# Sliding-window attention and a gated convolution FFN: keys as pairs of tokens, attention in 64x64 tiles of the array

## The chip, the core and the metric

The program runs on one NeuronCore of one Trainium2 chip. The time is the device time of one execution, in microseconds (us). Five engines work beside each other, each through its own instructions in program order: PE (TensorE: matrix products, with weight loads as PEld), DVE (VectorE), ACT (ScalarE), POOL (GpSimd) and SP (SyncE, which here issues the DMAs). Sixteen DMA engines move the data. Products land in PSUM, which this kernel uses as eight banks of 128 x 512 floats.

## The reference

```python
# q, k, v: (8 batches, 8 heads, 576 tokens, 64), f32
scores = q @ k.T / 8                       # per batch and head
scores = where(|i - j| <= 32, scores, -1e9)
attn   = exp(scores - max) / (sum + 1e-9)
x      = (attn @ v), heads side by side    # (8, 576, 512)
h      = relu(x @ w_in)                    # w_in: 512 x 1024
conv_t = sum over kk of conv_w[kk] * h[t + kk - 1]   # 3 taps, per channel, zero at the ends
out    = (h * sigmoid(conv)) @ w_out       # w_out: 1024 x 512; out: (8, 576, 512), f32
```

## The kernel before

All products are in bf16. Queries stand in tiles of 64 tokens, nine per batch. A tile's queries see only the 128 keys from 32 before it to 32 behind it. Two tiles that follow each other make a unit; there are 36 units, of which units 4 and 6 are worked as two halves (4a, 4b, 6a, 6b). The FFN goes in 12 chunks of 384 tokens, three per two batches of 576.

The order of the work is written out by hand: `PLAN` is a list of step names, and each step emits its instructions on its engines in that order. A name may carry the PSUM banks after @ and the engine after / (A for ACT, D for DVE, P for POOL, S for SP). The steps are:

- `LQK`, `CQK`, `TR`, `EV`: load q or k, cast it to bf16 (`qkb`), transpose it on PE, copy it out of PSUM (`qkT`). Head dimensions stand on 64 partitions, two head groups e = 0, 1 above each other.
- `LV`, `CV`, `VO`: load v in five pieces of 128 tokens per batch (`vst`), cast it (`ve`; a 65th column of ones gives the sums), and copy it with a shift of 64 tokens (`vo`), since an odd tile's 128 keys begin in the middle of a piece.
- `SC`, `EX`, `MA`, `AV`, `NO`: a unit's scores (keys on 128 partitions, queries along the row), exponential on ACT, mask on DVE, values product, and norm on DVE (a reciprocal and a multiplication, for each of two head groups).
- `XT`, `XE`: transpose x on PE and copy it to `xT`. From unit 20 on (`UD = 20`; units count from 0) the 16 units to the end have `XD` instead, a DMA transpose on SP's queue.
- `PH`, `RE`: hidden products of a chunk, eight of 128 channels, and relu on ACT to `hh`.
- `RO`: rows of `hh` rotated by 32, 64 or 96 partitions, by DMA or by DVE copies (`RO.2`).
- `CO`, `TA`, `GA`: the convolution as 32x32 diagonal products on PE, tanh on ACT, gate on DVE (`gT`). CO c.0 and c.1 are the two halves of chunk c.
- `YY`, `YC`, `YS`: output products, copy out of PSUM, store.
- `F`: products with zeros on PE that keep it busy while the first loads come.

Every engine copy goes through `copy`, every product through `mm` or `turn_mm`, so the profile puts them on those helpers' lines (L368, L370, L372; L378; L381). One instruction per engine waits for whatever its data need, and everything behind it on that engine waits too. An `LV` waits until the cast of the same piece of the batch before has freed its place in `vst`.

Tile size in this text means the part of PE's array that a product uses: 128*128 (hidden, output, x), 64*128 (scores; transposes of q and k), 128*64 (values), 32*32 (convolution). The rows of the profile print it.

Of the kernel before, what the change touches and what calls it, by code (L numbers as in the profile page):

```python
# [12 lines left out]
ALU = mybir.AluOpType  # L13
# [8 lines left out]
UD = 20  # L22
# [48 lines left out]

def build(k):
# [22 lines left out]
    def load_qk(b, parts):  # L95
        early = b < HB
        for z in parts:
            for y in range(2):
# [6 lines left out]
                add(f"TR{b}.{y}{z}", {"PE": 0.32}, lambda e, a=(q, ps): k.turn(*a), r=[("qkb", q)], w=ps, alloc=ps, mode="r64")  # L105
# [4 lines left out]
    def load_v(b):  # L110
        for c in range(5):
            add(f"LV{b}.{c}", {"SP": 0.58}, lambda e, a=(b, c): k.load_v(*a), w=[("vst", c)],
                size=1.32 if 0 < c < 4 else 1.05, desc=1024 if 0 < c < 4 else 768)
            add(f"CV{b}.{c}", {"POOL": 0.6} if b > 1 else {"POOL": 0.6, "DVE": 0.35, "ACT": 0.5},
                lambda e, a=(b, c): k.cast_v(e, *a), r=[("vst", c)], w=[("ve", b % 2, c)], port=1)
        for cs in [(c,) for c in range(4)] if b == 0 else [(0, 1, 2, 3)]:
            for h in range(2):
                add(f"VO{b}.{h}{cs[0]}", {"DVE": 0.06 + 0.14 * len(cs)}, lambda e, a=(b, h, cs): k.shift_v(e, *a),
                    r=[("ve", b % 2, c + h) for c in cs], w=[("vo", b % 2, c, h) for c in cs], port=1)

    def attend(u, tls):
# [3 lines left out]
        for t in tls:  # L125
            b, lt = (2 * u + t) // 9, (2 * u + t) % 9
            for hf in range(2):
                if b >= HB or (lt < 5, lt > 3)[hf]:
                    qk += [("qkT", b % 2, y, hf, x) for y in range(2) for x in range(2)]
            vs += [("vo", b % 2, lt // 2, h) for h in range(2)] if lt % 2 else [("ve", b % 2, lt // 2)]  # L130
        nm = f"{u}" + ("" if len(tls) == 2 else "ab"[tls[0]])
        ps = [Slot(), Slot()]
        add(f"SC{nm}", {"PE": 0.3 * f}, lambda e, a=(u, tls, ps): k.scores(*a), r=qk, w=ps, alloc=ps, mode="r64")
        for g in range(2):
            add(f"EX{nm}.{g}", {"ACT": 0.05 + 0.427 * f}, lambda e, z=(u, tls, ps[g], a, g): k.exp(*z),
                r=[ps[g]], w=[("attn", a, g)], uses=[ps[g]])
        add(f"MA{nm}", {"DVE": 0.06 + 0.54 * f}, lambda e, z=(u, tls, a): k.mask_(*z),
            r=[("attn", a, 0), ("attn", a, 1), "mk"], w=[("attn", a, 0), ("attn", a, 1)], port=1)
        ps = [Slot(), Slot()]
        add(f"AV{nm}", {"PE": 0.3 * f}, lambda e, z=(u, tls, ps, a): k.values(*z),  # L140
            r=[("attn", a, 0), ("attn", a, 1)] + vs, w=ps, alloc=ps, mode="c64")
        for g in range(2):
            add(f"NO{nm}.{g}", {"DVE": 0.54}, lambda e, z=(u, tls, ps[g], x, g): k.norm(*z),
                r=[ps[g]], w=[("xn", x, g)], uses=[ps[g]])
        if u >= UD:
            add(f"XD{nm}", {"SP": 1.22}, lambda e, z=(u, x): k.turn_x_dma(*z), r=[("xn", x, 0), ("xn", x, 1)],
                w=[("xT", u // 9 % 2, 2 * (u % 9) + t) for t in tls], size=1.3, desc=512)
            return
        ps = Slot()
        add(f"XT{nm}", {"PE": 0.24}, lambda e, z=(u, tls, ps, x): k.turn_x(*z),  # L150
            r=[("xn", x, 0), ("xn", x, 1)], w=[ps], alloc=[ps], mode="f")
        add(f"XE{nm}", {"DVE": 0.34, "ACT": 0.48}, lambda e, z=(u, tls, ps): k.evac_x(e, *z),
            r=[ps], w=[("xT", u // 9 % 2, 2 * (u % 9) + t) for t in tls], uses=[ps])
# [7 lines left out]
    def ffn(c):  # L161
        kind = c % 3
        for j in JORD:
            for g in range(2):
                m = 2 * j + g
                for half in (0, 1) if c == 1 else (None,):
                    lo, hi = span(c, half)
                    xs = [("xT", c // 3 % 2, t) for t in range(lo // 64, (hi - 1) // 64 + 1)]
# [39 lines left out]
    add("MK", {"DVE": 2.4}, lambda e: k.consts(), w=["mk"])  # L208
# [28 lines left out]
LQK0.10 LQK0.00 LQK0.11 MK LQK0.01 CQK0.10/A LV0.2 F512@0 F512@0 F512@0 F512@0 F512@0 F512@0 F512@0 F512@0 F512@0  # L237
F512@0 TR0.10@01 LV0.3 EV0.100/A EV0.101/D LV0.1 CQK0.00/D F512@2 F512@2 F512@2 TR0.00@10 CQK0.11/P EV0.000/D
EV0.001/A F512@2 SC0@10 TR0.11@23 LQK1.10 EX0.0 SC1@45 EV0.110/D EV0.111/A CQK0.01/P EX1.1 EX1.0 F512@6 F512@6
TR0.01@52 LQK1.00 EV0.010/D EV0.011/A EX0.1 LV0.0 F512@6 SC3@52 CW@4 MA0 LWI2 EX3.0 SC2@03 DG LV0.4 SC4a@16 EX2.1  # L240
LWI3 EX3.1 CV0.2/D EX2.0 VO0.11 CV0.3/A MA3 LWI0 CQK1.10/A MA1 LWI1 MA2 CV0.1/A F512@7 F512@7 F512@7 F512@7 F512@7
F512@7 F512@7 F512@7 F512@7 F512@7 F512@7 F512@7 F512@7 F384@7 TR1.10@02 VO0.03 VO0.12 EV1.100/A VO0.02 CQK1.00/D
F512@7 F512@7 F256@7 AV2@43 EV1.101/A VO0.10 EX4a.0 VO0.01 TR1.00@05 CV0.0/A NO2.0 AV1@12 EX4a.1 VO0.00 EV1.000/A
NO2.1 F384@7 AV0@64 EV1.001/A NO1.1 XT2@3 NO1.0 SC6a@50 EX6a.1 CV0.4/P NO0.0 F512@7 F128@7 XT1@1 SC5@02 CWI2/P XE1/A
SC4b@67 EX5.0 VO0.13 XE2/A CWI3/D LQK1.11 F512@1 F512@1 F128@1 AV3@01 EX5.1 MA4a EX4b.0 NO0.1 EX4b.1 LV1.0 NO3.1
F512@3 F512@3 F512@3 F512@3 XT0@4 LV1.3 NO3.0 AV4a@17 NO4a.1 XT3@0 XE0/D XE3/A CWI1/D EX6a.0 F512@3 F512@3 F512@3
F384@3 PH0.4@0 CWI0/P NO4a.0 LQK1.01 PH0.2@5 CQK1.11/P PH0.6@1 RE0.2 LV1.1 RE0.4 PH0.3@4 LV1.4 MA4b PH0.0@0 CV1.0/P
LV1.2 RE0.3 CV1.3/A PH0.1@5 MA5 RE0.6 MA6a AV4b@47 LV2.3 PH0.7@6 NO4b.1 LWO2 NO4b.0 TR1.11@12 CQK1.01/P XT4a@7
EV1.110/A EV1.111/D LWO1 XT4b@4 XE4a/A XE4b/D F512@3 F512@3 F128@3 TR1.01@21 RE0.1 LQK2.10 PH1.3a@7 RE0.0 EV1.011/D
EV1.010/A PH1.4a@5 RO0.1 CV1.4/P PH1.0a@0 CV1.1/A SC8@21 RE1.0a SC6b@43 EX8.0 CV1.2/D EX8.1 F512@0 F256@0 SC7@02  # L250
VO1.10 RE1.3a PH0.5@1 EX7.1 VO1.00 EX6b.0 PH1.6a@2 EX6b.1 MA8 EX7.0 AV5@47 MA6b PH1.5a@3 RE0.7 NO5.1 RE1.6a PH1.1a@0
RO0.3 RE1.5a NO5.0 AV6b@62 RE1.4a RE0.5 AV6a@37 PH1.2a@5 NO6b.0 XT5@1 LWO0 NO6a.1 PH1.7a@4 XE5/A NO6a.0 RE1.7a
F512@6 F128@6 AV8@67 RE1.1a MA7 RE1.2a XT6a@3 LWO3 CO0.0@5041 CWO1/P NO8.0 XE6a/A NO6b.1 AV7@63 TA0.03 NO8.1
PH1.5b@2 TA0.00 LQK2.00 NO7.1 CQK2.10 TA0.01 PH1.6b@7 RE1.5b NO7.0 RE1.6b XT6b@3 XT8@2 LQK2.11 GA0.01 CV2.3 XE6b/A
PH1.4b@7 XT7@6 XE8/D TA0.02 PH1.3b@0 RO0.2/D XE7/A PH1.1b@3 PH1.0b@2 RE1.4b RE1.1b GA0.00 PH2.4@6 RE1.0b RE1.3b
GA0.02 CO0.1@2537 GA0.03 PH1.2b@4 CWO0/P TA0.10 PH2.7@1 TA0.11 GA0.10 RE1.2b PH1.7b@0 TA0.12 CWO2/P GA0.11 RO1.1
PH2.3@4 RE2.4 GA0.12 RE2.7 PH2.6@5 RE1.7b CWO3/P TA0.13 RO1.3 PH2.5@0 GA0.13 CO1.0@1362 RE2.5 LQK2.01 RE2.6
TR2.10@07 CQK2.00 LV2.1 TA1.00 YY0.2@5 RE2.3 LV2.0 GA1.00 EV2.101/A EV2.100/D TA1.02 TA1.03 LV2.2 RO1.2/D CO1.1@0714
# [60 lines left out]
class Kernel:  # L319
# [54 lines left out]
    def fill(self, n, at):  # L374
        self.mm(self.banks[at][:, 0:n], self.zz[:, 0:128], self.zz[:, 0:n], start=True, stop=True)
# [343 lines left out]
```

## Time and profile before

| | us |
|---|---|
| three runs: median (lowest to highest) | 232.76 (232.06 to 235.51) |
| profiled execution: its time | 233.4 |
| profiled execution: span from first to last instruction | 231.7 |
| PE, DVE, ACT, POOL busy | 210.8, 173.3, 166.4, 64.4 |
| mean granted TensorE clock | 0.978 of full |
| DMA: data moved, share of 16 engines on the main queue | 48.80 MB, 78.2% |

Busy is the union of an engine's instructions. PE's instructions carry their way through the array, so that a busy PE may still have room, and two that follow each other overlap; steps on PE are better read from start to start. A row of the grouped views has line, engine, operation, output<-input, shapes and count, then busy us and mean ns of one, then the idle time ahead of it and what ended it. Some matmul records are missing from the trace, a few per cent.

### The profile page before, as it was taken

To read this page: it belongs to the slowest core of one execution; us is meant where nothing else is said; L and a number is where in the kernel's file an instruction comes from. 1 tells how busy PE (TensorE), PEld (TensorE's weight loads), DVE (VectorE), ACT (ScalarE), POOL (GpSimd) and SP (SyncE) were. 2 spreads that over 40 slices of the span, in tenths; PEclk is the share of its full clock that TensorE was granted. 3 is DMA by queue.
4 is the path that set the end of the run, shared out by engine and by line. 5 is a ranking of instruction groups with operands and counts; after the bars stand their busy time and mean duration, and the time that the engine had idled before them with its cause. 6 is when DMAs were issued, how large, how long until landed. Compare 5 with 4: busy or idle time off the path is not lost.

```text
span 231.7 us, 8843 instructions
## 1 busy us (share of the span) xinstructions
PE 210.8 (91%) x3705; PEld 122.0 (53%) x3737; DVE 173.3 (75%) x407; ACT 166.4 (72%) x365; POOL 64.4 (28%) x75
## 2 busy tenths in 40 slices
PE   7479898979999899899999999799899999899994
PEld 2354655756454665555455656455454655445543
DVE  7358874986779899958969888957799888643631
ACT  3366857867886899677796989798826877656861
POOL 2110443046345530555345114114043020000000
PEclk9957999999999999999999999999999999999999
DMA  5999949998899899994994696697996933621435
GB/s 161 321 267 266 296 108 229 236 274 257 218 280 316 244 226 340 257 273 122 344 329 67 208 236 202 171 229 120 362 221 109 260 132 79 190 57 37 160 118 201
DMA packets 67180, 49.38 MB, mean 213 GB/s; under 512 B 48044, under 2 KB 53444, under 8 KB 67140
## 3 DMA queue, kind: packets, MB, share of 16 engines
q1 hardware_dynamic: 67104, 48.80, 78.2%
q8 instruction: 29, 0.48, 0.9%
q14 instruction: 11, 0.09, 0.1%
q10 hardware_dynamic: 36, 0.01, 0.0%
HBM read 32.52 MB, written 9.44 MB: 181 GB/s over the span
## 4 chain that ended last, share of the span: by engine, by line
PE 49%; DVE 15%; DMA 12%; ACT 11%; issue 6%; SPq 4%; POOL 2%; DVEq 0%; ACTq 0%; POOLq 0%
PE ps L378 46%; ACT attn L520 6%; DMA hh<-hh 6%; DVE attn L528 4%; DMA vst<-in_v_dram 4%; DVE xn L549 4%; PE ps L381 3%; DMA st<-in_k_dram 3%; SPq L436 2%; ACT hh L596 2%; ACT qkT L368 2%; DVE gT L636 1%; DVE hh L370 1%; POOL ve L372 1%; DVE qkT L370 1%
## 5 line engine op out<-in xcount | busy, mean ns | idle before, releaser
L378 PE MATMUL ps<-xT,w_in_sb 128*128 128x385 bf16 (+2 forms) x416 | 70.6, 315 | 3.8 <-DVE gT L636 2.8
L378 PE MATMUL ps<-w_out_sb,gT 128*128 128x512 bf16 (+1 forms) x270 | 65.2, 373 | 1.7 <-issue 0.3
L636 DVE SCALAR_TENSOR_TENSOR gT<-ps,hh 128x384 bf16<-128x384 f32 x96 | 47.9, 549 | 16.9 <-ACT ps L629 12.6
L596 ACT ACTIVATE hh<-ps 128x385 bf16<-128x385 f32 (+2 forms) x104 | 45.9, 486 | 13.7 <-PE ps L378 13.3
L378 PEld LDWEIGHTS <-w_in_sb 128*128 128x128 bf16 x416 | 37.8, 98 | 28.3 <-issue 6.2
L372 POOL TENSOR_SCALAR qkb<-st 128x1152 bf16<-128x1152 f32 x28 | 33.6, 1208 | 66.3 <-DMA st<-in_q_dram 27.7
L629 ACT ACTIVATE ps<-ps 128x384 f32<-128x384 f32 x96 | 41.2, 487 | 12.6 <-PE ps L378 12.3
L378 PEld LDWEIGHTS <-gT 128*128 128x128 bf16 x296 | 27.2, 98 | 29.1 <-issue 0.9
L520 ACT ACTIVATE attn<-ps 128x512 bf16<-128x512 f32 (+1 forms) x76 | 39.2, 596 | 3.7 <-PE ps L378 3.4
L372 POOL TENSOR_SCALAR ve<-vst 128x512 bf16<-128x512 f32 x33 | 23.8, 728 | 43.4 <-DMA vst<-in_v_dram 40.9
L549 DVE TENSOR_TENSOR xn<-ps,rec 128x256 bf16<-128x256 f32 (+1 forms) x76 | 32.2, 424 | 2.6
L368 ACT COPY qkT<-ps 128x576 bf16<-128x576 bf16 x39 | 23.9, 651 | 11.5 <-PE ps L381 10.1
L528 DVE TENSOR_TENSOR attn<-attn,masks 128x1024 bf16<-128x1024 bf16 (+1 forms) x38 | 27.7, 744 | 5.8 <-ACT attn L520 5.4
L368 ACT COPY y<-ps 128x512 f32<-128x512 f32 (+1 forms) x29 | 16.8, 591 | 11.6 <-PE ps L378 10.2
L370 DVE COPY qkT<-ps 128x576 bf16<-128x576 bf16 x25 | 18.3, 750 | 8.2 <-PE ps L381 5.6
L378 PE MATMUL ps<-hh,diag 32*32 32x384 bf16 x1152 | 20.4, 327 | 1.8 <-DVE xn L549 1.1
L378 PE MATMUL ps<-zz 128*128 128x512 bf16 (+3 forms) x49 | 16.5, 464 | 2.5 <-DVE zz L385 1.3
L378 PEld LDWEIGHTS <-diag 32*32 32x32 bf16 x1152 | 11.7, 88 | 10.7 <-issue 7.7
L381 PE MATMUL ps<-ident,qkb 64*128 64x64 bf16 x576 | 13.6, 195 | 3.9 <-POOL qkb L372 1.3
L548 DVE RECIPROCAL rec<-ps 128x4 f32<-128x4 f32 (+1 forms) x76 | 13.2, 173 | 5.0 <-PE ps L378 4.7
L378 PEld LDWEIGHTS <-attn 128*64 128x64 bf16 x576 | 12.6, 110 | 8.1 <-issue 4.2
L381 PEld LDWEIGHTS <-qkb 64*128 64x128 bf16 x576 | 10.8, 97 | 11.4 <-issue 5.0
(51 smaller groups left out, 136.6 us busy)
## 6 DMA issues: line engine op xcount, KB each, us to landing
out_dram<-y SPq DMA_DIRECT2D x11, 768.0 KB, 4.9
st<-in_k_dram SPq DMA_DIRECT2D x12, 576.0 KB, 7.2
st<-in_q_dram SPq DMA_DIRECT2D x12, 576.0 KB, 6.9
vst<-in_v_dram SPq DMA_DIRECT2D x24, 256.0 KB, 6.5
vst<-in_v_dram SPq DMA_DIRECT2D x16, 192.0 KB, 6.0
hh<-hh SPq DMA_DIRECT2D x16, 144.8 KB, 3.6
st<-in_k_dram SPq DMA_DIRECT2D x8, 288.0 KB, 4.5
st<-in_q_dram SPq DMA_DIRECT2D x8, 288.0 KB, 5.0
```

Source lines behind the costliest of these rows:

```text
L368: self.do(nc.scalar.copy(out=out, in_=in_))
L370: self.do(nc.vector.tensor_copy(out=out, in_=in_))
L372: self.do(nc.gpsimd.tensor_scalar(out=out, in0=in_, scalar1=1.0, scalar2=0.0, op0=ALU.mult, op1=ALU.add))
L378: self.do(self.nc.tensor.matmul(*a, **kw))
L381: self.do(self.nc.tensor.transpose(out=out, in_=in_, identity=ident))
L520: self.do(self.nc.scalar.activation(at[:, lo:hi], self.ps(ps)[:, lo:hi], AF.Exp, bias=0.0, scale=self.scale))
L528: self.do(self.nc.vector.tensor_tensor(out=at, in0=at, in1=m, op=ALU.mult))
L548: self.do(self.nc.vector.reciprocal(rec, po[:, :, 64]))
L549: self.do(self.nc.vector.tensor_tensor(out=self.xn[x][lo:hi, 4 * g:4 * g + 4, :], in0=po[:, :, 0:64], in1=rec[:, :, None].broadcast_to([hi ...
L596: self.do(self.nc.scalar.activation(o, i_, AF.Relu, bias=0.0, scale=0.5))
L629: self.do(self.nc.scalar.activation(z, z, AF.Tanh, bias=0.0, scale=1.0))
L636: self.do(self.nc.vector.scalar_tensor_tensor(out=o, in0=z, scalar=1.0, in1=self.taps(kind, 0, 128, 6 + 2 * j + g if j else g, 1), op0=ALU ...
```

## The change

Five things change together.

1. V is loaded as pairs of tokens: a partition holds two tokens that follow each other, 512 bytes per head in one piece, and a batch comes in 3 loads instead of 5. `ve` then has keys of a tile on 64 partitions in two slots (even and odd token).
2. The shifted copy `vo` is made in four pieces of 32 partitions per batch instead of two of 64. `k_from` gives the place that each piece comes from.
3. `half` gives the half of the partitions on which a tile's keys stand. Scores, values and all transposes of q, k and x use 64x64 tiles of the array: `SC` and `AV` issue 32 products per unit instead of 16, `TR` 36 instead of 18, `XT` 16 of 64 x 64 instead of 4 of 128 x 128. The exponentials and masks keep 128 x 512 and 128 x 1024 for a whole unit; a half unit now has 64 partitions and full length. Values add two products (slots) in PSUM. Norms go by tile, not by head group.
4. `UD` and `XD` are gone: every unit is transposed on PE and copied out of two banks, by two `XE` of 128 x 256 instead of one of 128 x 512.
5. `PLAN` is new throughout: order, banks and engines of the copies. Fill products go from 55 to 30. `XE` is 40 times on DVE and 36 on ACT (before: 10 and 12), `YC` 13 times on DVE (before 8), `RO.2` four times on SP instead of DVE (chunks 5, 6, 8 and 10).

The masks and constants at the start are built for the new layout (six selects on POOL into space of `gT`).

```diff
+def k_from(o, hv, lo):
+    m = 1 - hv + lo
+    return (m + o) // 2, (m + o) % 2
...
     def load_v(self, b, c):
-        lo = 128 * c - PAD
-        s0, s1 = max(0, lo), min(S, lo + 128)
-        self.do(self.nc.sync.dma_start(self.vst[s0 - lo:s1 - lo, c], self.v_[b, :, s0:s1, :].rearrange("h p d -> p h d")))
+        lo = 256 * c - PAD - 128 * (b % 2)
+        s0, s1 = max(0, lo), min(S, lo + 256)
+        self.do(self.nc.sync.dma_start(
+            self.vst[(s0 - lo) // 2:(s1 - lo) // 2, c], self.v_[b, :, s0:s1, :].rearrange("h (p s) d -> p h (s d)", s=2),
+        ))
...
-    def shift_v(self, e, b, h, cs):
-        if h == 0:
-            self.copy(e, vo[0:64, c0:c1], ve[64:128, c0:c1])
-        else:
-            self.copy(e, vo[64:128, c0:c1], ve[0:64, c0 + 1:c1 + 1])
+    def shift_v(self, e, b, hv, lo, cs):
+        at, sh = k_from(b % 2, hv, lo)
+        c0, c1 = cs[0], cs[-1] + 1
+        w, r = 64 * hv + 32 * lo, 64 * sh + 32 * (1 - lo)
+        self.copy(e, self.vo[b % 2][w:w + 32, c0:c1], self.ve[b % 2][r:r + 32, c0 + at:c1 + at])
...
     def scores(self, u, tls, ps):
+        for pr in range(4):
+            for sl in range(2):
+                for tl in tls:
+                    b, t = (2 * u + tl) // 9, (2 * u + tl) % 9
+                    z = 64 * self.half(u, tl)
+                    for e in range(2):
+                        kT = self.qkT[b % 2][64 * e:64 * e + 64, 1, pr, 64 * t:64 * t + 128].rearrange("p (i s) -> p s i", s=2)
+                        self.mm(
+                            self.ps(ps[e])[z:z + 64, 256 * sl + 64 * pr:256 * sl + 64 * pr + 64], kT[:, sl],
+                            self.qkT[b % 2][64 * e:64 * e + 64, 0, pr, PAD + 64 * t:PAD + 64 * t + 64],
+                            start=True, stop=True,
+                        )
...
     def values(self, u, tls, ps, a):
+                    for e in range(2):
+                        self.mm(
+                            self.ps(ps[i])[64 * e:64 * e + 64, 65 * pr:65 * pr + 65], self.attn[a][z, e, sl, pr, :],
+                            v[:, 4 * e + pr, sl, :], start=(sl == 0), stop=(sl == 1),
+                        )
...
     def turn_x(self, u, tls, ps, x):
+        for tl in tls:
+            for pr in range(4):
+                for e in range(2):
+                    z = slice(64 * e, 64 * e + 64)
+                    w, at = 64 * (pr % 2), 128 * (pr // 2) + 64 * tl
+                    self.turn_mm(self.ps(ps[e]).bitcast(BF16)[w:w + 64, at:at + 64], self.xn[x][z, tl, pr, :], self.ident[z, z])
...
-    def turn_x_dma(self, u, x):
```

How the order moves, at three places. First PE between the scores of unit 17 and the values of unit 15, ahead of chunk 3's convolution (`qkT` is the transposed q and k, `attn` the masked exponentials, `ve` and `vo` the two copies of v; the size at the end is the product's output). Before:

```order
L378 LDWEIGHTS qkT_78
L378 MATMUL ps_114<-qkT_78 128x64
L378 LDWEIGHTS qkT_78
L378 MATMUL ps_117<-qkT_78 128x64
L378 LDWEIGHTS attn_86
L378 MATMUL ps_113<-vo_76,attn_86 64x65
L378 LDWEIGHTS attn_86
L378 MATMUL ps_113<-ve_74,attn_86 64x65
```

And now, where the values of unit 13 end and the scores of unit 17 begin:

```order
L392 MATMUL ps_116<-ve_73,attn_84 64x65
L392 LDWEIGHTS attn_84
L392 MATMUL ps_113<-ve_74,attn_84 64x65
L392 LDWEIGHTS attn_84
L392 MATMUL ps_113<-ve_74,attn_84 64x65
L392 LDWEIGHTS qkT_78
L392 MATMUL ps_115<-qkT_78 64x64
L392 LDWEIGHTS qkT_78
L392 MATMUL ps_118<-qkT_78 64x64
```

Scores have outputs of 64 partitions now, and between values and scores the tile size no longer changes. Second, DVE behind chunk 2's gates (`gT`), where batch 3's shifted copies, masks (`attn`) and norms (`rec`, `xn`) stand. Before:

```order
L636 SCALAR_TENSOR_TENSOR gT_100<-ps_114,hh_97 128x384
L370 COPY vo_76<-ve_74 64x2080 x2
L528 TENSOR_TENSOR attn_85<-attn_85,masks 128x1024
L548 RECIPROCAL rec_103<-ps_116 128x4
L549 TENSOR_TENSOR xn_89<-ps_116,rec_103 128x256
L548 RECIPROCAL rec_104<-ps_114 128x4
L549 TENSOR_TENSOR xn_89<-ps_114,rec_104 128x256
L528 TENSOR_TENSOR attn_84<-attn_84,masks 128x1024
```

Now (one more of the four shifted copies stands a few rows ahead, between two gates):

```order
L663 SCALAR_TENSOR_TENSOR gT_100<-ps_116,hh_97 128x384
L381 COPY vo_76<-ve_74 32x2080 x2
L562 TENSOR_TENSOR attn_86<-attn_86,masks 128x1024
L381 COPY vo_76<-ve_74 32x2080
L562 TENSOR_TENSOR attn_84<-attn_84,masks 128x1024
L562 TENSOR_TENSOR attn_85<-attn_85,masks 128x1024
L583 RECIPROCAL rec_105<-ps_120 128x4
L584 TENSOR_TENSOR xn_90<-ps_120,rec_105 128x256
```

Two copies of V have become four of the same length. Third, SP's queue behind the first eight loads of q and k (`st`). Before:

```order
L447 DMA vst<-in_v_dram 128x8x64 x3
L436 DMA st_64<-in_k_dram 128x1x576 x2
L436 DMA st_63<-in_q_dram 128x1x576 x2
L447 DMA vst<-in_v_dram 96x8x64
L461 DMA st_66<-in_moe_w_in_dram 128x4x256
L447 DMA vst<-in_v_dram 96x8x64
L461 DMA st_61<-in_moe_w_in_dram 128x4x256
```

And now:

```order
L473 DMA vst<-in_v_dram 48x8x128
L473 DMA vst<-in_v_dram 112x8x128
L473 DMA vst<-in_v_dram 128x8x128
L462 DMA st_64<-in_k_dram 128x1x576 x2
L488 DMA st_66<-in_moe_w_in_dram 128x4x256
L462 DMA st_63<-in_q_dram 128x1x576 x2
L488 DMA st_65<-in_moe_w_in_dram 128x4x256
```

All of batch 0's V now stands ahead of batch 1's q and k.

More of the change, by code (lines that the diff above doesn't have):

```diff
@@ L139, in attend @@
+        add(f"AV{nm}", {"PE": 0.3 * f}, lambda e, z=(u, tls, ps, a): k.values(*z),
+            r=[("attn", a, 0), ("attn", a, 1)] + vs, w=ps, alloc=ps, mode="s")
+        for t, p in zip(tls, ps):
+            add(f"NO{nm}.{t}", {"DVE": 0.54}, lambda e, z=(p, x, t): k.norm(*z),
+                r=[p], w=[("xn", x, t)], uses=[p])
         ps = [Slot(), Slot()]
-        add(f"AV{nm}", {"PE": 0.3 * f}, lambda e, z=(u, tls, ps, a): k.values(*z),
-            r=[("attn", a, 0), ("attn", a, 1)] + vs, w=ps, alloc=ps, mode="c64")
+        add(f"XT{nm}", {"PE": 0.24}, lambda e, z=(u, tls, ps, x): k.turn_x(*z),
+            r=[("xn", x, t) for t in tls], w=ps, alloc=ps, mode="s")
@@ L142, in attend @@
         for g in range(2):
[L143 to L151, printed above, removed]
@@ L316 @@
+YC11.2b/A YS11.2b YC11.2a/A YS11.2a
 """
@@ L677 @@
         name, _, eng = word.partition("/")
-        if not started and not name.startswith("L"):
+        if not started and not name.startswith("LQ"):
             kn.start()
```

344 lines of the change are left out of this document (172 added, 172 removed).

## The prediction

> **What bounds the kernel now.** I read the page first (busy shares and slices), then the stretches, to see each stage's margin, then TensorE's timeline for prices. The page's header, three rows by engine, the slices of TensorE, its clock and the DMA engines, and the chain by engine:
>
> ```profile
> span 231.7 us, 8843 instructions
> ...
> PE 210.8 (91%) x3705; PEld 122.0 (53%) x3737; DVE 173.3 (75%) x407; ACT 166.4 (72%) x365; POOL 64.4 (28%) x75
> ...
> PE   7479898979999899899999999799899999899994
> ...
> PEclk9957999999999999999999999999999999999999
> DMA  5999949998899899994994696697996933621435
> ...
> PE 49%; DVE 15%; DMA 12%; ACT 11%; issue 6%; SPq 4%; POOL 2%; DVEq 0%; ACTq 0%; POOLq 0%
> ```
>
> TensorE is busy 91% and holds half of the chain; VectorE and ScalarE come next with nearly equal load, and the DMA engines are full until two thirds of the span. I cut the span at 46.8 us (first convolution, CO0.0), at 58.8 and 162.0 (VectorE's first gate of chunk 1 and of chunk 7) and at 217.5 (first gate of chunk 11). Columns: stretch, length, then busy us of PE, PEld, DVE, ACT, POOL, granted clock, DMA share, GB/s.
>
> ```profile
> 0.00:46.80 46.80, 39.12 (x563) 23.42 (x569) 32.24 (x95) 29.70 (x62) 10.42 (x17) 0.89 0.91 237
> 46.80:58.80 12.00, 10.86 (x246) 7.43 (x245) 8.31 (x23) 8.63 (x25) 7.03 (x7) 1.00 0.92 250
> 58.80:162.00 103.20, 98.37 (x1920) 56.69 (x1936) 87.09 (x188) 84.35 (x182) 40.44 (x44) 1.00 0.88 234
> 162.00:217.50 55.50, 51.51 (x882) 28.86 (x889) 40.25 (x94) 37.96 (x86) 6.52 (x7) 1.00 0.59 155
> 217.50:231.70 14.20, 10.90 (x101) 5.58 (x101) 5.39 (x11) 5.74 (x13) 0.00 (x0) 1.00 0.51 182
> ```
>
> The middle (103.2 us) is TensorE's: 95% busy, while VectorE has 16.1 us to spare and ScalarE 18.9. The start is no engine's own; it waits for loads and short chains.
>
> **TensorE's part of the change.** These rows follow each other on TensorE's timeline (start, duration, shape, count; durations carry some 0.2 us of pipeline, so I go by starts):
>
> ```profile
> 91.26 0.41 PE L378 MATMUL ps<-qkT 64*128 64x64 bf16 x16
> 91.59 0.22 PE L378 MATMUL ps<-vo,attn 128*64 128x65 bf16 x1
> 91.60 0.22 PE L378 MATMUL ps<-ve,attn 128*64 128x65 bf16 x1
> ...
> 91.84 0.20 PE L378 MATMUL ps<-ve,attn 128*64 128x65 bf16 x1
> 91.97 0.34 PE L378 MATMUL ps<-xT,w_in_sb 128*128 128x385 bf16 x1
> ...
> 126.45 2.14 PE L378 MATMUL ps<-xT,w_in_sb 128*128 128x385 bf16 x12
> 128.43 0.39 PE L381 MATMUL ps<-ident,xn 128*128 128x128 bf16 x4
> 128.75 0.70 PE L381 MATMUL ps<-ident,qkb 64*128 64x64 bf16 x36
> 129.38 0.81 PE L378 MATMUL ps<-hh,diag 32*32 32x384 bf16 x48
> 130.14 0.39 PE L381 MATMUL ps<-ident,xn 128*128 128x128 bf16 x4
> ```
>
> Twelve hidden products start 1.98 us before the transposes of x behind them: 0.165 each, and both use the whole array, so nothing is lost between them. Four transposes to the next tile size take 0.32; at 0.055 each (128 columns against 385) that is 0.22 of work and **0.10 for the switch** of tile size. 36 transposes of q and k take 0.63, less 0.10 is 14.7 ns each, or 29 ns for a round of two tiles. 16 values products start within 0.25 us in 8 rounds, 31 ns a round. Scores take 0.33 less 0.10: 8 rounds again.
>
> In the new form scores, values and the transposes of q and k each have twice as many products in rounds of four instead of two: rounds stay 8, 8 and 9. If four tiles run beside each other, their time stays. This is the step that the trace doesn't show for 64x64; the nearest row is the convolution's, where 48 products in 16 tiles take 0.76 us with a switch, although 48 x 0.16 one after another would be 7.7. So I take rounds of four at 29 to 31 ns. A unit's transposes of x go from 0.22 to 4 rounds, 0.12; but 16 units that used a DMA transpose now use TensorE: 22 x 0.2 = 4.4 us (two split units at about half) become 38 x 0.12 = 4.6. Nothing.
>
> Switches, counted along the program's order, fall from 167 to 138: start 51 to 36, middle 83 to 66, end 33 to 36. That is 29 x 0.10 = **-2.9 us**, 1.7 of it in the middle, and 0.3 us more at the end. Warm-up products fall from 25,728 to 14,976 columns; they stand where TensorE waits in the start, so I count nothing for their time, and at most +2 us if the clock (5 tenths in its lowest slice) is granted later.
>
> **VectorE's and ScalarE's part.** Rows by form, mean ns before the bar:
>
> ```profile
> L370 DVE COPY vo<-ve 64x2080 bf16<-64x2080 bf16 x14 | 11.6, 827 | 2.5 <-POOL ve L372 2.1
> L370 DVE COPY xT<-ps 128x512 bf16<-128x512 bf16 x9 | 3.6, 413 | 0.5 <-PE ps L381 0.5
> L370 DVE COPY xT<-ps 128x256 bf16<-128x256 bf16 x1 | 0.3, 282 | 0.0
> L370 DVE COPY y<-ps 128x512 f32<-128x512 f32 x8 | 5.5, 683 | 6.0 <-PE ps L378 6.0
> L370 DVE COPY hh<-hh 64x772 bf16<-64x772 bf16 x16 | 7.8, 487 | 0.9 <-ACT hh L596 0.6
> L370 DVE COPY qkT<-ps 128x576 bf16<-128x576 bf16 x25 | 18.3, 750 | 8.2 <-PE ps L381 5.6 <-PE ps L378 2.4
> L549 DVE TENSOR_TENSOR xn<-ps,rec 128x256 bf16<-128x256 f32 x68 | 28.8, 424 | 2.3
> L549 DVE TENSOR_TENSOR xn<-ps,rec 64x256 bf16<-64x256 f32 x8 | 3.4, 422 | 0.3
> L528 DVE TENSOR_TENSOR attn<-attn,masks 128x1024 bf16<-128x1024 bf16 x34 | 26.3, 783 | 5.8 <-ACT attn L520 5.4
> L368 ACT COPY xT<-ps 128x512 bf16<-128x512 bf16 x9 | 5.3, 593 | 5.6 <-PE ps L381 5.5
> L368 ACT COPY xT<-ps 128x256 bf16<-128x256 bf16 x3 | 1.1, 374 | 0.4 <-PE ps L381 0.4
> L368 ACT CAST qkb<-st 128x1152 bf16<-128x1152 f32 x2 | 2.3, 1163 | 2.1 <-DMA st<-in_k_dram 2.1
> ```
>
> The shifted copies of V are now four of 32 partitions per batch, with the same 2080 columns as the two of 64. No row shows 32 partitions at that length; the norm's pair shows that half the partitions save nothing (424 and 422), so I take 827 each (bounds: 414, if the time went with the partitions, and 827). Between its first gates of chunks 1 and 7 VectorE's order holds, before and after: shifted copies 10 and 21 (+9.1 us), copies of xT 7 and 20 (7 x 0.413 to 20 x 0.282: +2.8), copies of qkT 14 and 16 (+1.5), masks 20 and 21 (+0.8), rotation copies 12 and 8 (4 x 0.487: -1.9). Sum **+12.3**: 87.1 becomes 99.4 of 103.2 us. With 414 for the copies it would be some 90. ScalarE gains 10 xT copies there (4 x 0.593 to 14 x 0.374: +2.9) and loses 4 of qkT and 2 exponentials: about even. Before chunk 1's gates, counted in the same way, VectorE gains some 4 us and ScalarE some 6 (three more casts of q and k at 1.163 make 3.5 of it, two casts of w_in most of the rest); at the end ScalarE gains 2.
>
> **DMA.** V comes in 24 transfers instead of 40, in 512-byte pieces instead of 256, and the 16 transposes are gone. What that can give is bounded by the waits that a DMA ends on the path. Of these the waits show one, and V's landing is not late for VectorE beyond the second:
>
> ```profile
> DVE gT L636 <- DMA hh<-hh: 3.7, 3, 1.6
> DVE vo L370 <- POOL ve L372: 2.1, 4, 0.6
> PE ps L378 <- DVE gT L636: 3.2, 4, 1.1
> ```
>
> TensorE itself waits 3.2 us for gates, so faster transfers are worth 0 to 3.7 us; four rotations that move from VectorE to SP's queue (chunks 5, 6, 8, 10) add 8 transfers there, each with a gate of its chunk queued behind its landing. SP loses 16 transposes and 16 V loads in exchange. I take 0.
>
> **Added waits.** Odd tiles' values now wait for copies out of up to four instructions, queued on VectorE among masks and norms; behind them stand the gates, for which the output products wait. That is the place where VectorE's 12 us would show.
>
> **The sum**, against the profiled execution (233.4 us, 1.7 beside the span; the median of 232.8 is 0.6 below it). Start: ScalarE's extra casts against V's earlier place in the queue and the switches, 0 (-2 to +3). Middle: TensorE's need falls by 1.7, VectorE's own busy time alone makes 99.4. The two stretches with the densest VectorE work are these:
>
> ```profile
> 60.00:80.00 20.00, 18.80 (x385) 10.74 (x389) 17.63 (x40) 15.47 (x33) 9.95 (x12) 1.00 1.04 276
> 80.00:100.00 20.00, 19.34 (x386) 11.42 (x388) 18.10 (x39) 17.50 (x39) 5.71 (x6) 1.00 0.98 275
> ```
>
> 35.7 of 40 us, 89%, with TensorE still at 95%. At 89% the middle would take 99.4 / 0.89 = 111.7; at 100% it isn't lengthened. With both ends possible I take the mean, 105.5: **+2.3**. End: -1 to +1, 0. Together 235.7, and 235 on the median's footing: +1.0%, inside the 2% that a measurement of this kernel can tell.
>
> **Rivals.**
> - *VectorE becomes the bound in the middle* (slower): price 111.7 - 103.2 = 8.5, so 241. It decides as soon as VectorE can't be kept over 94% busy beside TensorE. For it: 89% is the most that the trace shows over 40 us. Against: nothing there shows it as a limit.
> - *The waits were the loss, and they go* (faster): -2.9 for switches, -3.7 for rotated rows, up to -2 in the start, if VectorE's copies fill its idle 16 us: 233.4 - 0.6 - 8.6 = 224, or 227 without half of it. For it: full DMA slices until 140 us. Against: TensorE waits only 4.8 us in the middle.
> - *Rounds of four don't run beside each other* (much slower): each takes two rounds' time: (38 + 38 + 32) x 0.25 + 38 x 0.12 = 31.6 us of TensorE's path, 264. The convolution's row speaks against. Here a rule of the Trainium skill bears on it: "TensorE: Matmul & The Clock Gate", Weight-path perf modes, says that fast weight loading is on when 128 weights are loaded, so 64-column loads would lose it. Values products load 64 columns now and keep 31 ns a round against 29, so by that rule the sum gains 70 x 8 x 2 ns, about 1 us. The same page (Part 1, on the 56 ns gap) gives a floor of about 25 ns from start to start; by it 2,216 more products would cost 55 us. The two products of a values round in the trace start within 0.01 us of each other, which speaks against that floor between tiles.
>
> **Chances.** Forecast (230 to 238.5) 0.52; VectorE bound 0.22 (238 to 244); waits go 0.21 (223 to 229); rounds split 0.05. The range leaves out the last and the outer part of the two before: 226 to 243. Faster by over 2% (under 228.1): 0.19 of the third and the forecast's edge, 0.20. Slower (over 237.4): 0.20 + 0.05 + 0.02 = 0.27. The rest, 0.53, lies within.
>
> **What would show it.** Scores, values and transposes with starts 7 to 8 ns apart within a round's mean show the tiles side by side; 14 would show the third rival. VectorE's busy time near 190 us and its 32-partition copies near 0.8 us show that term; 0.4 would take away half of it. First gate of chunk 1 near 59 us and of chunk 7 near 164 show where time went; gates waiting for rotated rows under 2 us show the DMA's relief. The forecast fails if the new order lets VectorE run over 95% busy (then the faster rival), or if a queue that I counted at nothing, SP's or ScalarE's start, holds up TensorE.

## The result, and the profile after

The changed kernel took 277.44 us (median of four runs, 275.07 to 280.42) against 232.44 for the kernel before on the same chip: a ratio of 1.187, 95% interval 1.171 to 1.203. The forecast was 235.0 with a range of 226 to 243. Medians here are of all runs, ratios of the undisturbed ones alone, since some executions of most kernels are over 1.5% slower than the kernel's fastest. The page of the profiled execution after, in the rows shown of before (span; busy time; slices of PE, granted clock and DMA; the chain), and its DMA queues:

```profile
span 274.4 us, 13282 instructions
PE 226.5 (83%) x5928; PEld 131.1 (48%) x5928; DVE 194.0 (71%) x438; ACT 176.1 (64%) x388; POOL 64.1 (23%) x65
PE   6667469749978797677988699994999989999995
PEclk9657559986997999979999899997999999999999
DMA  6999916891799379786199318399011070142416
q1 hardware_dynamic: 40352, 47.50, 59.8%
q8 instruction: 46, 0.75, 1.2%
PE 59%; DVE 17%; issue 15%; ACT 4%; DMA 3%; SPq 1%; DVEq 0%; ACTq 0%
```

TensorE is busy a smaller share of a longer span (83% against 91%), with holes in its slices until two thirds of it. No engine took its place: VectorE has 71%. In the chain DMA and ScalarE gave way to TensorE's own work (49% to 59%) and to "issue", from 6% to 15%: time in which an engine waited for nothing that the profile names. The queue of instructions, q8, carries 46 packets; before it carried:

```profile
q8 instruction: 29, 0.48, 0.9%
```

0.75 MB in 46 packets is 16 KB each. A product is two instructions, weight load and matmul: 11,856 after (5,928 products) and 7,474 before (3,737). Divided by 46 and by 29 packets, both give 258. So q8 brings TensorE its program in blocks of 256 instructions, or 128 products.

The stages after, cut at the same events (CO0.0, the first gates of chunks 1, 7 and 11; columns as before):

```profile
0.00:54.03 54.03, 37.86 (x1040) 22.41 (x1040) 36.53 (x92) 35.46 (x66) 12.93 (x22) 0.72 0.81 220
54.03:71.91 17.88, 14.11 (x332) 10.32 (x326) 10.97 (x28) 10.07 (x31) 6.38 (x6) 0.81 0.64 153
71.91:204.96 133.05, 110.48 (x3145) 62.90 (x3143) 100.90 (x210) 87.17 (x193) 44.84 (x37) 0.95 0.69 201
204.96:260.79 55.83, 53.73 (x1322) 30.18 (x1322) 39.61 (x101) 39.30 (x92) 0.00 (x0) 1.00 0.28 91
```

The start lost 7.2 us, the next stage 5.9, the middle 29.9, and the later stages nothing. The granted clock fell too, in the start from 0.89 to 0.72. From 50 us on the trace has it fall to 0.50 five times, each time at a stall of TensorE of 2.4 to 4.1 us, and never at one of 1.0 to 1.7.

The waits of TensorE after (who waited for what: us in total, times, longest), and TensorE's groups of 64x64 products:

```profile
PEld L392 <- issue: 52.4, 125, 4.0
PEld L395 <- issue: 22.9, 30, 3.9
PE ps L392 <- issue: 19.0, 13, 3.8
PE ps L395 <- issue: 14.6, 7, 3.8
...
L395 PE MATMUL ps<-ident,qkb 64*64 64x64 bf16 x1152 | 17.4, 203 | 13.4 <-issue 10.3 <-ACT qkb L379 3.1
L392 PE MATMUL ps<-qkT 64*64 64x64 bf16 x1152 | 19.0, 205 | 8.9 <-issue 7.9 <-DVE xn L584 0.8 <-ACT attn L555 0.2
L392 PE MATMUL ps<-vo,attn 64*64 64x65 bf16 x512 | 15.4, 202 | 3.4 <-issue 3.4
L395 PE MATMUL ps<-ident,xn 64*64 64x64 bf16 x576 | 12.0, 204 | 4.6 <-issue 4.2 <-DVE xT L381 0.2
```

The two rows of PE are the ones that grew; before, the row of L378, where most of its products stand, was

```profile
PE ps L378 <- issue: 1.6, 7, 0.3
```

The rows of PEld (weight loads) say less: before, "PEld L378 <- issue" already had 28.9 us in 87 waits.

Where such a wait stands is seen on TensorE's timeline at 182 us, two steps of 36 transposes of q and k with other work between:

```profile
182.25 0.48 PE L395 MATMUL ps<-ident,qkb 64*64 64x64 bf16 x36
182.55 0.22 PE L392 MATMUL ps<-ve,attn 64*64 64x65 bf16 x2
...
184.79 0.32 PE L395 MATMUL ps<-ident,xn 64*64 64x64 bf16 x16
185.13 0.34 PE L395 MATMUL ps<-ident,qkb 64*64 64x64 bf16 x18
189.27 0.47 PE L395 MATMUL ps<-ident,qkb 64*64 64x64 bf16 x18 [3.80 <-issue]
```

The first step runs through in 0.30 us. The second stops in its middle, though its first half ran and both halves need the same data and banks, for 3.8 us. It is product 4,062; counted from the start of the program, 15 of the 19 gaps of over 1 us between starts stand at products 94, 222, 350 and so on, 128 apart: the ends of blocks. In the trace's packets of q8 the block that begins there is fetched from 186.76 to 187.81, after TensorE entered the block before it at 182.09, and TensorE goes on 1.46 us after it landed. Where the DMA engines are idle a fetch begins about 1 us after the block before it was entered; where they are full it takes 3 to 5. Then come some 1.1 us for the packet and 1.2 to 1.6 until the next product. A block that is used up sooner than that stalls TensorE. Before, a block lasted 4.7 to 11.4 us; after, 128 small products can be gone in 1.5 to 4.

To put a size on it: for each block end, the time over the three starts around it, less the median of such threes nearby, summed. That is **39.0 us after and 1.5 before** (in the start 12.2, in the next stage 3.9, in the middle 22.4, later 0.6). Without it the runs stand at 238.4 and 230.9. Counted in the same way at other places in the cycle of 128, where no block ends, the two runs give mostly 1 to 5 us and at most 7.5. How far "nearby" reaches moves a figure by 1 to 4 us. So figures of 20 and more are time at block ends, and figures below 5 can't be told from none.

### The profile page after: what moved, and what is told of

It is laid out like the page before. It is cut to its first block, busy times and chain, and to the rows that moved or that the text cites. A ratio compares the mean times of both kernels' runs of the same rounds, so it can differ in the third digit from the quotient of the medians.

```text
span 274.4 us, 13282 instructions
## 1 busy us (share of the span) xinstructions
PE 226.5 (83%) x5928; PEld 131.1 (48%) x5928; DVE 194.0 (71%) x438; ACT 176.1 (64%) x388; POOL 64.1 (23%) x65
## 4 chain that ended last, share of the span: by engine, by line
PE 59%; DVE 17%; issue 15%; ACT 4%; DMA 3%; SPq 1%; DVEq 0%; ACTq 0%
PE ps L392 53%; PE ps L395 6%; DVE vo L381 3%; DVE xn L584 3%; DVE attn L562 3%; DVE gT L663 3%; DMA st<-in_k_dram 2%; DMA hh<-hh 1%; DVE qkT L381 1%; ACT qkT L379 1%; ACT attn L555 1%; DVE rec L583 1%; DVE hh L381 1%; DVE xT L381 1%; SPq L462 1%
## 5 line engine op out<-in xcount | busy, mean ns | idle before, releaser
L392 PE MATMUL ps<-w_out_sb,gT 128*128 128x512 bf16 (+1 forms) x296 | 70.5, 388 | 1.1 <-DVE gT L663 0.9
L383 POOL TENSOR_SCALAR ve<-vst 128x1024 bf16<-128x1024 f32 (+1 forms) x22 | 24.4, 1112 | 63.1 <-DMA vst<-in_v_dram 38.4
L583 DVE RECIPROCAL rec<-ps 128x4 f32<-128x4 f32 x72 | 12.7, 176 | 29.3 <-PE ps L392 26.8
L584 DVE TENSOR_TENSOR xn<-ps,rec 128x256 bf16<-128x256 f32 x72 | 30.6, 425 | 2.5
L381 DVE COPY vo<-ve 32x2080 bf16<-32x2080 bf16 (+1 forms) x36 | 27.3, 758 | 2.0 <-POOL ve L383 1.1
L395 PE MATMUL ps<-ident,qkb 64*64 64x64 bf16 x1152 | 17.4, 203 | 13.4 <-issue 10.3
L392 PE MATMUL ps<-qkT 64*64 64x64 bf16 x1152 | 19.0, 205 | 8.9 <-issue 7.9
L395 PEld LDWEIGHTS <-qkb 64*64 64x64 bf16 x1152 | 14.0, 114 | 20.1 <-issue 13.4
L392 PEld LDWEIGHTS <-qkT 64*64 64x64 bf16 x1152 | 15.6, 117 | 12.5 <-issue 12.0
L392 PEld LDWEIGHTS <-attn 64*64 64x64 bf16 x1152 | 14.7, 113 | 12.4 <-issue 10.1
```

The lines of the kernel that those rows point to most:

```text
L381: self.do(nc.vector.tensor_copy(out=out, in_=in_))
L383: self.do(nc.gpsimd.tensor_scalar(out=out, in0=in_, scalar1=1.0, scalar2=0.0, op0=ALU.mult, op1=ALU.add))
L392: self.do(self.nc.tensor.matmul(*a, **kw))
L395: self.do(self.nc.tensor.transpose(out=out, in_=in_, identity=ident))
L583: self.do(self.nc.vector.reciprocal(rec, po[:, :, 64]))
L584: self.do(self.nc.vector.tensor_tensor(out=self.xn[x][:, t], in0=po[:, :, 0:64], in1=rec[:, :, None].broadcast_to([128, 4, 64]), op=ALU.mu ...
```

## The experiments

**Theories.** *Supply*: TensorE lacks instructions at block ends. *Tiles*: 64x64 rounds are slow in the array. *VectorE*: its 20 us more hold the middle. *Order*: the new order or its start. Later a fifth was needed: every added TensorE instruction costs the same wherever it stands.

**1. Wide products in the changed kernel.** In `turn`, `turn_x`, `scores` and `values`, two 64x64 products become one of 64x128; transposes give the same data, scores and values don't:

```diff
-                for e in range(2):
-                    self.turn_mm(...[64 * e:64 * e + 64, 64 * j:64 * j + 64], self.qkb[q][z, j, e], self.ident[z, z])
+                self.turn_mm(...[:, 64 * j:64 * j + 64], self.qkb[q][z, j].rearrange("p e d -> p (e d)"), self.ident[z, z])
```

> The changed kernel with its order, V layout, masks, shifted copies and DMAs, but the products of full units and all transposes take 64 rows by 128 columns again instead of 64 by 64, in the same rounds: about 3,976 products instead of 5,928. The scores and values it computes are not the reference's (the keys of the two slots are mixed); every instruction off TensorE keeps its shape. Supply theory (TensorE's program comes in blocks of 256 instructions, that is 128 products; a block is fetched only after the one before it was entered, and small products use a block up before the next has come): the stalls at block ends, some 38 us of the changed kernel's run, fall to about 8, so 235 to 250 us, likeliest 241, and the 'issue' share of the chain falls from 15% to 6 or 7%. Tile theory (rounds of four 64 by 64 tiles are themselves slow): 240 too, but then the mean starts within scores and values rows of the changed kernel should be 14 ns or more away from block ends, which they are not. VectorE theory (shifted copies and copies of xT hold the middle): 270 to 280. Order theory (the new order or its start is at fault): 270 to 280.

Measured: 239.46 us (239.37 to 244.2), ratio to before 1.034 (1.026 to 1.041). 38 of the 45 us went with nothing changed but the number of TensorE's products and their width. The page and the same three stages:

```profile
PE 215.2 (91%) x3976; PEld 121.3 (51%) x3976; DVE 191.4 (81%) x438; ACT 174.3 (73%) x388; POOL 65.2 (27%) x65
q8 instruction: 31, 0.51, 1.0%
...
0.00:45.43 45.43, 36.80 (x619) 20.63 (x620) 36.59 (x91) 35.02 (x66) 13.42 (x22) 0.77 0.92 254
45.43:57.78 12.35, 12.30 (x277) 8.37 (x272) 10.55 (x29) 9.88 (x31) 5.54 (x5) 1.00 1.03 247
57.78:169.66 111.88, 102.93 (x2035) 57.87 (x2034) 98.75 (x210) 86.52 (x193) 46.25 (x38) 0.98 0.80 238
```

VectorE's load is as after (191.4), and the start is shorter than before the change: order and VectorE are not the 38 us. Block ends cost 4.7 us here, and "issue" is 6% of the chain. Tiles would allow 240 as well, but its condition fails in the changed kernel's trace: away from block ends its scores and values start 8.7 and 8.9 ns apart at the median, not 14.

**2. Wide transposes alone**, same results (the edit above in `turn` and `turn_x`):

> The changed kernel with only its transposes of q, k and x in 64 by 128 tiles instead of pairs of 64 by 64: the same results, 5,064 products instead of 5,928. Supply theory: blocks last 1.17 times as long on the mean; with the fetch times of the changed kernel's run the stalls fall from 38 to about 22 us, so 255 to 268 us, likeliest 261. Tile theory: half of the 64 by 64 rounds that remain are as slow as before, so 265 to 270, with new switches between tile sizes. VectorE theory and order theory: 275 to 281.

Measured: 258.83 us (252.97 to 261.04; no interval came with it). The median lies between supply's bounds, the fastest run 2 us below them, and all four below tiles' 265. The trace, of a run of 260.3 us, has 39 blocks and 19.5 us at their ends.

**3. Split transposes in the kernel before** (the reverse edit, in `turn` alone):

> The kernel before with only its transposes of q and k split into 64 by 64 tiles (36 instead of 18 in a step, nine rounds of four instead of nine of two): 4,313 products instead of 3,737, the same results. Supply theory: blocks last 0.87 times as long; stalls appear at some of the transposes, 3 to 8 us more, 236 to 241 us. Tile theory, if a round of four takes the time of two rounds: 32 steps x 0.25 us = 8 us, 240. VectorE and order theories: 232, no change.

Measured: 241.04 us (238.07 to 243.93), ratio 1.034 (1.021 to 1.047). By its size it fits supply and tiles alike, but the trace speaks against tiles: a split step lasts 0.41 us from its start to the next step's, at the median, against 0.37 before (8.1 ns a product, or 32 ns a round of four, against 29 for two). That is 0.04 us a step where tiles asked for 0.25, or 1.3 us for 32 steps. Block ends cost 3.9 us, 2.4 more than before, which is within the scatter of the count; one stall of 0.79 us at 65.8 stands inside a step of split transposes. The larger part of the 8 us is not explained, neither by supply nor by tiles.

**4. The changed kernel without the later loads:**

```diff
-        else:
+        elif b < 3:
             src = self.qk[y][b, 2 * z:, :, :]
...
-        self.do(self.nc.sync.dma_start(
+        if b < 3: self.do(self.nc.sync.dma_start(
```

> The changed kernel with the loads of q, k and v of batches 3 to 7 left out (their casts read old data; the result is not the reference's). TensorE's program is untouched. Supply theory: a block's fetch waits behind data in the DMA queues (3 to 5 us where they are full, 0.7 to 1.7 where they are idle); with the fetch turn capped near 4 us the stalls after 80 us fall by some 20 us, so 245 to 262 us, likeliest 254. Tile theory: 277, since no product changes. VectorE theory: 277. Order theory: 275 to 280.

Measured: 261.60 us (260.56 to 262.31), ratio to before 1.129 (1.121 to 1.137): 15.8 us gone with TensorE's program untouched. The middle:

```profile
71.34:189.83 118.49, 106.51 (x3144) 61.64 (x3143) 102.59 (x211) 86.61 (x192) 45.37 (x37) 0.97 0.23 73
```

It lost 14.6 us as the DMA share fell from 0.69 to 0.23; block ends there cost 5.3 us instead of 22.4. In the start, whose loads are all there, they still cost 10.9. It gave less than the likeliest value since I had taken all fetches as quiet after 80 us, and some still met full DMA engines: one at 101 us began 4.7 us after the block before it was entered.

**5. The control: the kernel before without the same loads** (the same edit):

> The control: the kernel before without the loads of q, k and v of batches 3 to 7 (the result is not the reference's). In the changed kernel leaving them out took 15.8 us off. Supply theory: the kernel before has 1.5 us of stalls at block ends, so 229 to 233 us. If the loads cost time in another way (late data, contention for the memories) that both kernels share: 217 to 224.

Measured: 232.74 us (229.51 to 234.46), ratio 0.997 (0.991 to 1.003). The loads cost nothing that can be measured where blocks last long enough, so what experiment 4 won is not late data or contention that both kernels share. Its own count agrees: 18 us less at block ends.

**6. Rounds of four tiles by themselves** (the code is shortened):

```python
for i in range(count // 4):
    for r in range(2):
        for c in range(2):
            matmul(banks[bank + r][64*c:64*c+64, 0:cols], w[64*r:64*r+64, 64*c:64*c+64], x[64*r:64*r+64, 0:cols])
```

> TensorE alone, in rounds of four 64 by 64 tiles on zeroed data: 2,560 products of 64 columns, then 512 each of 128, 256 and 512 columns. SyncE loads q and k (18.9 MB) from the start, so that the first 65 us or so are under full DMA load and the rest is quiet; nothing else runs, and the output is zeros instead of the reference's. Supply theory: time goes by blocks of 128 products whatever their size: 5.5 to 7 us a block under load, 3.2 to 3.6 when it is quiet, for 64 and for 128 columns alike; at 256 columns the work itself takes about 3.4, so there is little or no gap; at 512 columns 6.8 and no gap. Tile theory: no pattern of blocks; a block of 64 columns takes 0.9 us if four tiles run beside each other and 1.9 to 3.8 if they don't, evenly, loaded or not, and time goes with the columns.

Measured: one execution, 179.7 us with the stores at its end. TensorE's timeline under load, then quiet, then with 128 and 256 columns (start, duration, count, the wait ahead; the last row runs on into the products of 512):

```profile
21.42 1.93 PE L57 MATMUL bank<-x,w 64*64 64x64 bf16 x128 [4.28 <-issue]
27.62 1.92 PE L57 MATMUL bank<-x,w 64*64 64x64 bf16 x128 [4.27 <-issue]
33.81 1.92 PE L57 MATMUL bank<-x,w 64*64 64x64 bf16 x128 [4.27 <-issue]
...
67.04 1.92 PE L57 MATMUL bank<-x,w 64*64 64x64 bf16 x128 [1.53 <-issue]
70.50 1.92 PE L57 MATMUL bank<-x,w 64*64 64x64 bf16 x128 [1.53 <-issue]
...
102.40 1.98 PE L57 MATMUL bank<-x,w 64*64 64x128 bf16 x128 [1.47 <-issue]
109.59 26.67 PE L57 MATMUL bank<-x,w 64*64 64x256 bf16 x693 [0.47 <-issue]
```

Exactly 128 products, then a wait. A block takes 6.20 us under full load and 3.46 to 3.73 when it is quiet, and 3.46 as well with twice the columns; from 256 columns on, where the work itself lasts 3.4 us (6.8 at 512), the waits are gone. The products are side by side: 13.3 ns each at the granted clock of 0.50, in both stretches of 64 columns:

```profile
15.23:46.21 30.98, 9.61 (x641) 8.94 (x641) 0.00 (x0) 0.00 (x0) 0.00 (x0) 0.50 1.05 390
60.13:88.31 28.18, 15.38 (x1024) 14.30 (x1024) 0.00 (x0) 0.00 (x0) 0.00 (x0) 0.50 0.02 5
...
98.95:109.59 10.64, 7.23 (x385) 6.68 (x385) 0.00 (x0) 0.00 (x0) 0.00 (x0) 1.00 0.02 5
```

The third row is of 128 columns: the same kind of waits, at a clock of 1.00.

The first wait comes after 223 products, about the second block end, so one block is on hand beyond the one that is being worked. In the trace's packets of q8 each of these waits ends 1.2 to 1.6 us after a block has landed. For such a stream this settles supply's mechanism and its two prices, and tiles falls.

**7. Shifted copies cut to one of eight heads,** on the changed kernel and on the wide one:

```diff
-        self.copy(e, self.vo[b % 2][w:w + 32, c0:c1], self.ve[b % 2][r:r + 32, c0 + at:c1 + at])
+        self.copy(e, self.vo[b % 2][w:w + 32, c0:c1, 0:1], self.ve[b % 2][r:r + 32, c0 + at:c1 + at, 0:1])
```

> The changed kernel with its shifted copies of V cut to one of eight heads (the result is not the reference's): some 20 us of VectorE's 194 go, 15 of them between the first gates of chunks 1 and 7; a memset on GpSimd comes in at the start. Supply theory: TensorE's stalls stand where its blocks end, so 270 to 278 us, likeliest 275. VectorE theory (its load or its queue holds the middle): 258 to 266. Order theory: 272 to 278.

> The changed kernel with wide products (64 rows by 128 columns, the run that gave 239.5 us) and with its shifted copies cut to one of eight heads as well: what is left of the 7 us between that run and the kernel before. If the rest is VectorE's added load: 232 to 235 us. If it is the order, the start and the stalls that remain: 237 to 240.

Measured: 269.81 us (267.46 to 275.3), ratio to before 1.164 (1.148 to 1.180). That lies between the two ranges, 0.2 us below supply's and 4 above VectorE's; block ends cost 36.3. The edit took less than expected: a thin copy still takes 342 ns, and VectorE's total fell by 12.8 us, not 20. In the middle 10.0 us of VectorE's work went (100.90 to 90.89), and the stage became 2.1 us shorter:

```profile
68.45:199.42 130.97, 109.51 (x3124) 62.88 (x3139) 90.89 (x210) 86.24 (x190) 42.38 (x37) 0.93 0.70 204
```

On the wide kernel 239.46 (236.19 to 240.93), ratio to before 1.026 (1.007 to 1.046) against the wide run's 1.034: no gain that can be told from noise. So VectorE's load is not the 45 us; whether it holds a part of the last 7 is not settled, since this run had 8.8 us at block ends against the wide run's 4.7.

**8. Long products split in two,** in the kernel before: output and hidden products together, then each alone (hidden products likewise):

```diff
-        for m in range(MB):
-            self.mm(self.ps(ps)[:, lo:hi], ..., self.w_out[:, m, lo:hi], ...)
+        for a, b in ((lo, mid), (mid, hi)):
+            for m in range(MB):
+                self.mm(self.ps(ps)[:, a:b], ..., self.w_out[:, m, a:b], ...)
```

> The kernel before with every hidden and output product split into two of half the columns: some 700 products more (4,440 in all), more than the split transposes added, and the same results; but these take 0.08 to 0.11 us each, so a block of 128 lasts 10 us or more. Supply theory: no stalls, 232 to 236 us (a few ns at each start). A theory in which every added TensorE instruction costs the same wherever it stands: the split transposes cost 8.3 us for 576 products, 14 ns each, so 700 would cost 10 us, 243. VectorE, order theories: 232 to 234.

Measured: 241.66 us (241.19 to 244.03), ratio 1.048 (1.035 to 1.060). A miss for supply: 9 us slower although block ends cost no more than before (1.4). The fifth theory fits, so each half was run alone.

> The kernel before with only its output products split in two halves of the columns: 288 products more in stretches of 0.11 us each, the same results. Supply theory: no stall at block ends; 0.5 us of columns, so 232 to 235 us. If every added TensorE instruction costs some 13 ns wherever it stands (the 9.3 us of both splits over 700 products): 236 to 237. If the output split alone made those 9 us: 240 or more.

> The kernel before with only its hidden products split in two halves of the columns: 416 products more, 0.08 us each, the same results. Supply theory: no stall at block ends; 1.2 us of columns, so 233 to 236 us. 13 ns for each added instruction: 238 to 239. If the hidden split alone made the 9 us: 240 or more.

Measured: output alone 233.45 us, ratio 1.003 (0.998 to 1.008); hidden alone 238.20, ratio 1.027 (1.019 to 1.035). 288 added products cost nothing that can be measured: by the upper end of the interval at most 6 ns each, half of what the fifth theory asks. Of the hidden split's 5 us, 1.2 are columns; 2.3 more at block ends is within the scatter of the count, and the rest I can't place. With both splits, nearly 4 us more than the two alone are open. So the kernel before loses some us to edits like these and that of experiment 3 in a way that no theory here explains.

**9. Wide and quiet:**

> The changed kernel with wide products and without the loads of q, k and v of batches 3 to 7 (neither part computes the reference's result): it asks what is left of the 7 us between the wide run (239.5 us) and the kernel before. Supply theory: 4.7 us of stalls at block ends were left there, of which some 3 go: 234 to 237. If transfers that land late were the rest: 230 to 233. VectorE or order: 237 to 240.

Measured: 243.46 us (241.48 to 245.09), ratio 1.048 (1.039 to 1.057), slower than the wide run and outside all three. Its timeline names one wait, and beside it VectorE and GpSimd at work just before:

```profile
78.57 0.23 PE L392 MATMUL ps<-ve,attn 64*128 64x65 bf16 x1 [4.02 <-DVE attn L574]
71.11 2.95 DVE L574 TENSOR_TENSOR attn<-attn,masks 128x1024 bf16<-128x1024 bf16 x2
66.71 5.38 POOL L383 TENSOR_SCALAR qkb<-st 128x1152 bf16<-128x1152 f32 x4
```

A values product waits 4.0 us for a mask on VectorE. Two masks take 2.95 us there; in the wide run (experiment 1) the same two took less than half, with GpSimd idle:

```profile
68.70 1.30 DVE L574 TENSOR_TENSOR attn<-attn,masks 128x1024 bf16<-128x1024 bf16 x2
```

GpSimd's casts of q, k and v no longer wait for loads here, and run on without a pause from 66.7 to 78 us beside VectorE's masks and copies. In five traces (before, changed, wide, and the two quiet ones of experiments 4 and 9) masks and copies take longer then: in the changed kernel's a mask takes 0.69 us on the mean where GpSimd works less than half of that time and 1.17 where it works more, a shifted copy 0.71 and 1.42. So the wide kernel can be held by VectorE and GpSimd at work together. That is a candidate for its last 7 us too, which stay open.

**Together.** Time at block ends, by the same count in each run:

| run | products | median us | at block ends | difference |
|---|---|---|---|---|
| before | 3,737 | 232.4 | 1.5 | 230.9 |
| before, quiet | 3,737 | 232.7 | 1.8 | 230.9 |
| before, split transposes | 4,313 | 241.0 | 3.9 | 237.1 |
| changed | 5,928 | 277.4 | 39.0 | 238.4 |
| changed, thin copies | 5,928 | 269.8 | 36.3 | 233.5 |
| changed, quiet | 5,928 | 261.6 | 21.0 | 240.6 |
| changed, wide transposes | 5,064 | 258.8 | 19.5 | 239.3 |
| changed, all wide | 3,976 | 239.5 | 4.7 | 234.8 |
| changed, all wide, thin copies | 3,976 | 239.5 | 8.8 | 230.7 |
| before, both long splits | 4,449 | 241.7 | 1.4 | 240.3 |

Times of the changed kernel from 239 to 277 us become 231 to 241 once block ends are taken off. They explain some 37 of the 45 us. In the kernel before with split products they explain little. The medians are of different chips; by the ratios, each against before on its own chip, the wide products won 36 us and the missing loads 13, in place of 38 and 15.8. No version tried beats the kernel before.

## Why the prediction was wrong

**The step that failed** is in TensorE's part: "rounds stay 8, 8 and 9. If four tiles run beside each other, their time stays." The condition held: the 36 transposes at 182.25 us take 0.30 us, 8.3 ns each, a round of four in 33 ns where I took 29 to 31 (34 to 36 at the median of all steps; for some 900 rounds that is an estimate of 4 us). The conclusion didn't. I counted the array's time and gave the program's 4,400 added instructions no price. The runs showed 39.0 us of waiting at the ends of instruction blocks in its place, against 1.5 before. What I named as a danger, "a queue that I counted at nothing", came true in a queue I had not listed: TensorE's own instructions. Part of it could be seen before: the page has the q8 row, and in the trace a next block landed up to 6.0 us after the one ahead of it was entered, while a block lasted 4.7 to 11.4 us. That would have shown how little room there was. The waits gave no warning: PE's "issue" row had 1.6 us.

The Trainium skill has the parts of it: "Runtime: NRT & Kernel Launch", Instruction fetch mechanics, says that an engine's program is refilled in blocks of 16 KiB, 256 instructions, over a DMA queue of its own. The 46 packets agree. It also says that the fetch is hidden, because instructions are dispatched more slowly than they are filled. The block of 128 products that ran 1.7 us and then waited 1.8 to 4.5 contradicts that for streams of small products.

**Third rival** (264 us, 0.05): nearest in time, wrong in mechanism. Starts are 8.4 to 8.9 ns apart at the median of the steps of scores, values and transposes, not 14. The floor of 25 ns from the Trainium skill's "TensorE: Matmul & The Clock Gate", Part 1, doesn't hold between tiles: 13.3 ns at half clock in experiment 6.

**VectorE's terms** held: copies of 32 partitions take 834 ns (827 taken), its total 194.0 ("near 190"), the middle's 100.9 (99.4). Its price stays uncertain: without block ends the middle is 110.7 us, 108.1 in the wide run, against my 105.5 and the rival's 111.7. My 105.5 was not a sound mean either: its lower end, 99.4, is VectorE's work alone and lies below TensorE's own need (103.2 less 1.7 for switches). With 101.5 there, it would have been 106.6. The 834 ns are a mean of two cases, copies beside a working GpSimd and copies without (experiment 9).

```profile
L381 DVE COPY vo<-ve 32x2080 bf16<-32x2080 bf16 x28 | 23.3, 834 | 0.7
L663 DVE SCALAR_TENSOR_TENSOR gT<-ps,hh 128x384 bf16<-128x384 f32 x96 | 47.8, 551 | 15.2 <-ACT ps L656 10.2 <-DMA hh<-hh 2.4 <-PE ps L392 2.3
```

**DMA relief**, taken as 0 of at most 3.7: the gates' waits for rotated rows went from 3.7 to 2.4 us (I had named under 2 as the sign), and leaving out most loads gave the kernel before nothing.

**Clock:** "at most +2 us if the clock is granted later" was for fewer warm-up products. The clock did fall, from 0.89 to 0.72 in the start. The wide run, with the same warm-up, has 0.77 there with next to no time at block ends, so the stalls are not the main cause of that fall; whether the warm-up is, no run shows. It cost little by itself, since the wide run's start is shorter than before.

**Start and end** (0 each): the end held (55.8 against 55.5); the start's +7.2 is 12.2 at block ends less some 5 that came back elsewhere in it. What the fewer switches of tile size won, 1.7 us by my count for the middle, no run measured.

## What to carry to other kernels

A product in a quarter of the array costs as many instructions as one in all of it. Before splitting products, divide the stretch's time by its instructions in blocks of 256 (128 products): where a block lasts less than some 3.5 us with quiet DMA, or 6 under full DMA load, TensorE will starve. Long products in the same block pay for short ones, and an "issue" wait of PE itself that returns every 128 products is the sign. A split that passes this test can still cost time: in experiments 3 and 8 three of four splits lost 5 to 9 us, of which block ends explain little.

## What the runs showed of the hardware that was not expected

- The fetch of TensorE's next block waits among the data packets: 4.5 us of gap under 390 GB/s of loads, 1.8 to 2.1 in quiet, for the same products.
- One block is fetched at a time, once the one before is entered: 128 products set the pace at 3.5 us whether they hold 64 or 128 columns.
- A starved TensorE at the low clock stayed there: 0.50 from 7.7 to 88.3 us of the rounds alone. At the high clock it kept that: 1.00 from 98.95 to 109.59 us, although waits of 1.05 to 1.47 us came back with each block of 128 columns. In the changed kernel, from 50 us on, it took stalls of 2.4 us and more to bring it down.
- VectorE's masks and copies took 1.7 and 2.0 times as long beside a working GpSimd (0.69 and 1.17 us, 0.71 and 1.42 us in the changed kernel).
- The loads of five batches (17.7 MB) cost the kernel before nothing (ratio 0.997) and the changed one 15.8 us by the medians, 13 by the ratios.
